# Crossbar DMA transposes, casting weight loads and a fixed program order on every engine, in a windowed-attention plus ResMLP kernel

## The chip, the cores and the metric

The kernel runs on one core of one Trainium2 chip. The metric is the device time in microseconds (us). A profiled span is about 1.7 us shorter than the time of the same run. A run counts as slow when it is over 1.5% above the fastest of the same kernel.

The engines are TensorE (PE in the profile), VectorE (DVE), ScalarE (ACT), GpSimd (POOL) and SyncE (SP, which here only issues DMAs).

## The reference

```python
# q, k, v: (8, 8, 576, 64); 8 global positions; window +-32
scores = q @ k.T / 8                      # per batch and head
mask   = |i - j| <= 32, or i global, or j global
x      = softmax(scores where mask) @ v   # -> (8, 576, 512)
u      = x + lam * (w_tok @ (alpha1*x + beta1))                  # token mixing, 576x576
out    = u + lam * (relu((alpha2*u + beta2) @ w_ch1) @ w_ch2)    # 512 -> 2048 -> 512
```

I call each of the eight batches an *image*. The MLP works on 9 groups of 512 flat rows ("mlp 0" to "mlp 8"). A group consists of four tiles of 128 rows. Image 0 completes four such tiles and image 1 completes five.

## The kernel before

TensorE executes in program order. The other engines are ordered by a scheduler. The attention of an image is latency-bound, so the MLP of an earlier image is interleaved as *filler*: the attention code yields a number, and that many MLP matmuls are issued. K, Q and the MLP input are turned by TensorE transposes and copied out of PSUM. `alpha2` and `lam` are multiplied into the weights.

```python
ctx.enter_context(tc.manual_schedule(engines={mybir.EngineType.PE}))
...
def front(b):                       # attention and token mixing of image b
    for p in range(4):
        ps = mm(BF16, 512)
        for c in range(4):          # four TensorE transposes of K
            T.transpose(out=ps[:, c*P:(c+1)*P], in_=kq16[:, 0, c, p*P:(p+1)*P], identity=identb)
        for hh in range(2):         # copied to KTz by VectorE
            V.tensor_copy(out=A(KTz, ...), in_=A(ps, ...))
        ps = sc(BF16)               # the same for Q, copied to QT by ScalarE
        ...
    # ... scores, exp, P@V, token mixing; then for each finished tile of 128 rows:
        SC.copy(out=u16, in_=U[f])
        # later: ut_tile(f): four transposes of u16, one VectorE copy to UT

def mlp(g):
    ...                             # ml <- W1 x UT, relu to HTb, ml <- HTb x W2
    V.tensor_tensor(out=u, in0=ps, in1=u, op=ALU.add)
    nc.sync.dma_start(out=outf[P*f : P*f+P, :], in_=u)

def w1_load():                      # fp32 staging, then scaled to bf16
    nc.sync.dma_start(out=r[:, 0:1024], in_=moe_w_ch1[...])
    V.tensor_scalar(out=W1[...], in0=r[...], scalar1=a2c[...], op0=ALU.mult)   # or ScalarE

for b in range(NB):
    for n in front(b):
        for _ in range(n):
            if b > 0: next(fill)
    done[0] = b + 1 if b < NB - 1 else 9     # which MLP groups are ready
```

The softmax here doesn't subtract the row's maximum and nothing guards it: scores larger than these inputs give would overflow.

## Time and profile before

The median is 469.44 us (469.03 to 470.72). The first lines are of the profile's page of the kernel before: busy time of TensorE with its share of the span, then the busy tenths in 40 slices of 11.7 us (9 is 90% or more) of TensorE and of the DMA engines, then the DMA queue that carries most, with packets, megabytes and share of the engines' time.

```profile
PE 410.1 (87%) x3779; PEld 232.9 (50%) x3779; DVE 234.1 (50%) x497; ACT 195.0 (42%) x344; POOL 176.6 (38%) x213
```

```profile
PE   0135488869999999999999999999999999999996
...
DMA  7972849994975083408330852171012001101101
```

```profile
q1 hardware_dynamic: 73008, 48.92, 37.0%
```

The digits show two stages. From the tenth slice on TensorE is full, and only fewer or shorter matmuls can help there. Before that it is idle for much of the time, and the order of loads and small operations decides. The table by stretches of the kernel before follows, as start:end and length, then busy microseconds and instructions of PE, PEld, DVE, ACT and POOL, then granted clock, DMA share and GB/s:

```profile
0.00:70.00 70.00, 28.54 (x325) 22.25 (x326) 41.88 (x94) 20.24 (x33) 48.29 (x65) 0.88 0.67 188
...
100.00:140.00 40.00, 37.60 (x351) 21.61 (x352) 21.21 (x46) 12.75 (x22) 19.81 (x24) 0.91 0.79 185
140.00:200.00 60.00, 58.99 (x606) 34.15 (x605) 31.01 (x69) 32.78 (x63) 25.83 (x31) 1.00 0.43 124
200.00:220.00 20.00, 20.00 (x204) 11.24 (x202) 10.33 (x23) 4.87 (x9) 10.81 (x13) 1.00 0.43 106
220.00:440.00 220.00, 216.28 (x1957) 119.33 (x1955) 107.75 (x230) 100.68 (x180) 56.34 (x68) 1.00 0.24 69
```

From 140 us on TensorE is idle for about 5 of 300 us, and the DMA engines have room (0.24 to 0.43). In the first 70 us TensorE works for 28.5 us. The list of waits of the kernel before (total us, times, longest) shows the first reasons: the gathered rows of the global tokens, and the casts of K.

```profile
PE mm L286 <- POOL kqn L280: 16.1, 1, 16.1
PE mm L297 <- DVE kq_101 L147: 8.5, 1, 8.5
```

The timeline of TensorE in the kernel before shows when the MLP starts (start, length, engine, line, operation):

```profile
78.04 1.44 PE L478 MATMUL ml<-UT,W_118 128*128 128x512 bf16 x3
```

So the MLP, which fills everything later, starts at 78.04 us.

| kernel before, profiled run | us |
|---|---|
| matmul work in all | 384.5 |
| lost until the first MLP matmul (78.0 us) | 56.7 |
| lost from there to 140 us | 13.4 |
| lost from 140 to 240 us | 3.6 |
| lost from 240 us on | 11.2 |

### The profile page before, as it was taken

What the parts mean: (1) busy time and instruction counts of PE and PEld (TensorE: products, weight loads), DVE (VectorE), ACT (ScalarE), POOL (GpSimd) and SP (SyncE); (2) the same over time, 40 slices, a digit from 0 to 9 for tenths busy, and PEclk for the clock granted to TensorE, in tenths of its full rate; (3) what the DMA queues carried; (4) which work ended last, traced back from release to release, by engine and by line L of the source; (5) the groups of instructions that cost most, each with busy time, mean ns of one, the idle gap of its engine ahead of it and who ended that gap; (6) DMA issues with size and microseconds to landing.
All of it is one profiled execution on the core that took longest, in us unless ns stands there. A gap on an engine that the chain in (4) does not pass through costs nothing.

```text
span 469.4 us, 9110 instructions
## 1 busy us (share of the span) xinstructions
PE 410.1 (87%) x3779; PEld 232.9 (50%) x3779; DVE 234.1 (50%) x497; ACT 195.0 (42%) x344; POOL 176.6 (38%) x213
## 2 busy tenths in 40 slices
PE   0135488869999999999999999999999999999996
PEld 0125454536556655664556456545655565444442
DVE  4635778625483548354736474556545554501001
ACT  1216412634158414831682268127712770370540
POOL 6448883825733465235414341524160023000000
PEclk9999667979999999999999999999999999999999
DMA  7972849994975083408330852171012001101101
GB/s 195 230 249 56 273 131 306 213 247 88 280 167 176 13 199 97 135 25 193 104 124 24 192 148 78 43 172 46 2 46 70 24 1 46 45 1 45 46 22 67
DMA packets 76440, 54.21 MB, mean 115 GB/s; under 512 B 49392, under 2 KB 66736, under 8 KB 76400
## 3 DMA queue, kind: packets, MB, share of 16 engines
q1 hardware_dynamic: 73008, 48.92, 37.0%
q0 software_dynamic: 2048, 4.66, 4.5%
q8 instruction: 29, 0.48, 0.4%
q10 hardware_dynamic: 1344, 0.07, 0.2%
q14 instruction: 11, 0.09, 0.1%
HBM read 39.27 MB, written 9.44 MB: 104 GB/s over the span
## 4 chain that ended last, share of the span: by engine, by line
PE 75%; POOL 7%; DMA 7%; DVE 6%; issue 3%; SPq 0%; ACT 0%; POOLq 0%; DVEq 0%; ACTq 0%
PE ml L487 26%; PE ml L478 24%; PE sc L455 8%; PE xps L380 4%; PE sc L328 4%; PE mm L358 3%; DVE KTz L299 3%; PE xps L381 2%; DMA vo<-ve 2%; DMA kq<-in_k_dram,hg_idx 2%; DMA R_94<-in_k_dram 1%; PE mm L443 1%; DMA R_94<-in_q_dram 1%; PE sc L410 1%; POOL W_119 L542 1%
## 5 line engine op out<-in xcount | busy, mean ns | idle before, releaser
L478 PE MATMUL ml<-UT,W_118 128*128 128x512 bf16 x576 | 155.4, 386 | 1.7 <-DVE U L491 1.7
L487 PE MATMUL ml<-W_119,HTb 128*128 128x512 bf16 x576 | 139.5, 379 | 0.0
L481 ACT ACTIVATE HTb<-ml,bias1T 128x512 bf16<-128x512 f32 x144 | 98.7, 687 | 31.8 <-PE ml L478 30.8
L487 PEld LDWEIGHTS <-HTb 128*128 128x128 bf16 x576 | 53.4, 98 | 56.5 <-issue 0.2
L478 PEld LDWEIGHTS <-W_118 128*128 128x128 bf16 x576 | 49.2, 99 | 39.7 <-issue 7.6
L335 ACT ACTIVATE Pt<-sc 128x432 f16<-128x432 f32 x96 | 50.1, 531 | 36.3 <-PE sc L328 17.5
L491 DVE TENSOR_TENSOR U<-ml,U 128x512 f32<-128x512 f32 x36 | 24.8, 689 | 61.2 <-PE ml L487 60.9
L392 POOL TENSOR_TENSOR XL_116<-x,LA_207 128x512 bf16<-128x512 f32 x16 | 20.3, 1269 | 76.6 <-DVE x L385 76.6
L456 DVE TENSOR_TENSOR U<-sc,x 128x512 f32<-128x512 f32 (+1 forms) x40 | 27.6, 690 | 35.3 <-PE sc L455 34.9
L299 DVE COPY KTz<-mm 64x512 bf16<-64x512 bf16 x64 | 44.0, 687 | 1.5 <-PE mm L297 0.3
L328 PEld LDWEIGHTS <-KTz 128*128 128x128 bf16 x576 | 32.2, 103 | 22.1 <-issue 3.1
L392 POOL TENSOR_TENSOR XL_115<-x,LA_207 128x512 bf16<-128x512 f32 x16 | 20.3, 1268 | 47.5 <-DVE x L385 47.4
L328 PE MATMUL sc<-QT,KTz 128*128 128x72 bf16 x576 | 36.0, 204 | 0.6 <-ACT Pt L335 0.5
L303 ACT COPY QT<-sc 128x512 bf16<-128x512 bf16 x32 | 18.6, 584 | 41.4 <-PE sc L302 40.8
L385 DVE TENSOR_TENSOR x<-xps,rden 128x640 f32<-128x640 f32 x32 | 26.4, 824 | 1.9 <-DVE rden L384 0.5
L455 PE MATMUL sc<-XL_116,wtT_122 128*128 128x512 bf16 x100 | 24.8, 379 | 0.0
L337 DVE TENSOR_TENSOR GRT_108<-Pt,grm 128x80 f16<-128x80 f16 x16 | 3.4, 212 | 43.0 <-ACT Pt L335 42.9
L455 PE MATMUL sc<-XL_115,wtT_121 128*128 128x512 bf16 x100 | 24.7, 379 | 0.0
L297 PE MATMUL mm<-identb,kq_101 128*128 128x128 bf16 x128 | 13.8, 237 | 12.0 <-DVE kq_101 L147 8.5
L380 PEld LDWEIGHTS <-PTz_106 128*128 128x128 f16 x288 | 16.9, 104 | 8.6 <-DMA vo<-ve 4.8
L380 PE MATMUL xps<-ve,PTz_107 128*128 128x65 f16 x160 | 16.6, 197 | 5.1 <-DVE x L385 5.1
L380 PE MATMUL xps<-vo,PTz_106 128*128 128x65 f16 x128 | 16.2, 203 | 4.6 <-DMA vo<-ve 4.6
(247 smaller groups left out, 557.7 us busy)
## 6 DMA issues: line engine op xcount, KB each, us to landing
out_dram<-U SPq DMA_DIRECT2D x36, 256.0 KB
vo<-ve POOLq DMA_DIRECT2D x16, 260.0 KB, 5.5
RV_99<-in_v_dram SPq DMA_DIRECT2D x16, 256.0 KB
R_94<-in_k_dram SPq DMA_DIRECT2D x4, 512.0 KB
R_95<-in_k_dram SPq DMA_DIRECT2D x4, 512.0 KB
R_96<-in_q_dram SPq DMA_DIRECT2D x4, 512.0 KB
R_97<-in_q_dram SPq DMA_DIRECT2D x4, 512.0 KB
RV_98<-in_v_dram SPq DMA_DIRECT2D x8, 256.0 KB
```

The costliest lines, as they stand in the source:

```text
L299: V.tensor_copy(out=A(KTz, 640 * (2 * p + hh) + 32, [[4, P], [1, 4]], 64 * hh, 64), in_=A(ps, 0, [[1, P], [P, 4]], 64 * hh, 64))
L328: T.matmul(out=ps[:, i * 144 + 72 * hh : i * 144 + 72 * hh + 72], lhsT=KTz[:, 2 * p + hh, 64 * t : 64 * t + P], rhs=QT[:, p, 72 * t : 72 * ...
L335: SC.activation(out=Pt[:, 432 * un : 432 * un + 432], in_=ps[:, 0:432], func=AF.Exp, bias=0.0, scale=0.125)
L380: T.matmul(out=o_, lhsT=ptz[:, base : base + P], rhs=vv, start=(i == 0), stop=False)
L385: V.tensor_tensor(out=A(x, P * p, [[64, 2], [DM, 5], [1, 64]]), in0=A(xps, 0, [[512, 2], [65, 5], [1, 64]]), in1=A(rden, 0, [[5, 2], [1, 5 ...
L392: G.tensor_tensor(out=A(xl, DM * full + P * p, [[DM, 4], [1, P]]), in0=A(x, DM * full + P * p, [[DM, 4], [1, P]]), in1=A(LA1, P * p, [[0, ...
L455: T.matmul(out=ps, lhsT=wtT[par][:, c, P * u : P * u + P], rhs=xl[:, c, :], start=(c == 0), stop=(c == 4))
L456: V.tensor_tensor(out=U[f][r0:r1, :], in0=ps[r0:r1, :], in1=x[r0:r1, u, :], op=ALU.add)
L478: T.matmul(out=ps, lhsT=W1[:, cc, ec * P : (ec + 1) * P], rhs=ut[:, cc, :], start=(cc == 0), stop=(cc == 3))
L481: SC.activation(out=HTb[:, slots[ec], :], in_=ps, func=AF.Relu, bias=bias1T[:, ec : ec + 1], scale=1.0)
L487: T.matmul(out=ps, lhsT=HTb[:, slots[ec], P * j : P * j + P], rhs=W2[:, ec, :], start=(ec == 0), stop=(ec == 15))
L491: V.tensor_tensor(out=u, in0=ps, in1=u, op=ALU.add)
```

## The change

The intent is to take the transposes off TensorE, to take the scaling of the weights off the other engines, and to fix every engine's order by hand so that image 0 runs as early as possible. The diff, cut to its core:

```diff
-ctx.enter_context(tc.manual_schedule(engines={mybir.EngineType.PE}))
+ctx.enter_context(tc.manual_schedule(engines={EN.PE, EN.DVE, EN.Activation, EN.Pool, EN.SP}))
-psM bufs=2, psL bufs=2
+psM bufs=1, psL bufs=3
@@ K and Q of images 1 to 7: loads in 256-byte rows, GpSimd casts, crossbar transposes
+def qk_chunk(b, c):
+    for i, src in enumerate((k, q)):
+        nc.sync.dma_start(out=A(r, 512*i, ...), in_=src[b, :, P*c:P*c+n, :].rearrange("h p d -> p h d"))
+    def cast(E): ...                 # to zero-padded kz and to q16
+def xbar_qk():
+    for c in range(5):
+        nc.sync.dma_start_transpose(out=A(KTz, 32+P*c, [[640, 8], [1, n]]), in_=kz[0:n, c, :])
+    nc.sync.dma_start_transpose(out=A(QT, 0, ...), in_=q16[0:64, ...])
+    nc.sync.dma_start_transpose(out=A(QT, 1600, ...), in_=q16[64:P, ...])
@@ MLP input
-                SC.copy(out=u16, in_=U[f])
-                wait.append((f, u16))        # four TensorE transposes and a copy later
+                V.tensor_tensor(out=u16, in0=U[f], in1=a2b, op=ALU.mult)
+                nc.sync.dma_start_transpose(out=UT[g][:, :, P*(f%4):P*(f%4)+P], in_=u16)
@@ output of the MLP
-            V.tensor_tensor(out=u, in0=ps, in1=u, op=ALU.add)
+            V.tensor_tensor(out=tmp, in0=ps, in1=lamb, op=ALU.mult)
+            V.tensor_tensor(out=u, in0=tmp, in1=u, op=ALU.add)
@@ weights: cast in the DMA, no scaling
-    (w1_load, w2_load: fp32 staging and scaling on VectorE, ScalarE, GpSimd)
+    G.dma_start(out=W1[:, :, 512*blk:512*blk+512], in_=moe_w_ch1[...])
+    G.dma_start(out=W2[:, 4*blk:4*blk+4, :], in_=moe_w_ch2[...])
@@ image 0 is written out by hand; it keeps TensorE transposes for K, Q (not for u16)
+done = [1]
+for _ in range(80):                # 80 MLP steps of mlp 0 before image 1
+    next(fill)
+for b in range(1, NB): ...         # 103 filler steps an image or more, before about 135
```

Who issues what is not free to choose. The Trainium skill, "DMA: Bandwidth & Descriptors", section "SWDGE vs HWDGE vs iDMA", says that only GpSimd can issue a DMA that casts, and only SyncE or ScalarE a plain DMA transpose. The change puts all transposes on SyncE, which also issues the loads of K, Q and V and the stores of the output.

## The prediction

> **What bounds it now.** The page: TensorE busy 410.1 of 469.4 us (87%); TensorE is 75% of the chain of work that ended last. The table by stretches separates two stages. From 108 us on TensorE is busy 97-100% of every stretch, so instruction count on TensorE decides there. Before that it idles: the timeline shows the first MLP matmul only at 78.0 us, and by 108 us TensorE has been busy about 60 us. By the waits and the timeline: kqn on GpSimd costs TensorE a 16.1 us wait, attention of image 0 starts at 35.8 us, VectorE and ScalarE scale W1 between its steps.
>
> **Removed.**
> 1. TensorE transposes. In dense stretches four 128-column ones advance the timeline 0.22 us and the eight small ones take 0.32 us: 8 x 0.22 + 0.32 = 2.1 us an image, 7 images, 15 us; the MLP input's 36 x 0.22 = 8 us. Together 23 us, all on the critical path.
> 2. Their evictions: VectorE KTz 64 x 0.69 and UT 36 x 0.42, ScalarE QT 32 x 0.58. Mostly off the path, but TensorE waits about 1 us at each image's head for KTz and QT (busy 1.4-1.5 of 2 us there): 6 us.
> 3. W1/W2 staging and scaling on VectorE, ScalarE and GpSimd, and the kqn detour. I expect attention of image 0 at about 20-22 us, mlp 0 at 62-66 us instead of 78: 13 us.
>
> **Added.**
> 1. Crossbar transposes: zero-padded K 1.18, Q 0.59, u16 0.59 MB an image, 2.36 MB. No trace shows one. The Trainium skill, "DMA: Bandwidth & Descriptors", section "Latency and other measured facts", states 261 GB/s effective: 9 us an image as an estimate.
> 2. K and Q of images 1-7 now load in 256-byte rows (1 KB before). V's 256-byte rows moved at 220-230 GB/s with the DMA share near 1.0, so 2.36 MB takes 10.5 us. With V 5, vo 2, output 4 us: about 31 us of DMA an image.
> 3. The filler schedule shrinks from about 135 to 101 MLP steps an image, so an image lasts about 35 us instead of 46, and pure MLP is left for the end (about 90 us instead of 45). DMA is then 85-90% loaded during images.
> 4. In image 1 mlp 1 isn't ready, so 48 of 101 steps are real; the rest of image 1 runs bare, at image 0's pace. I charge 8-10 us.
> 5. A second VectorE operation per output tile (0.69 us): off the path.
>
> **Sum.** 469.4 - 23 - 6 - 13 + 9 = 436; with the earlier indirect gathers 433 us, range 412 to 463. Faster by over 2%: 0.82; within 2%: 0.10; slower: 0.08.
>
> **What would show each step.** TensorE instructions fall by about 420, busy time to about 375-390 us, no transposes after the prologue. First MLP matmul at 60-67 us. A gap in TensorE's busy tenths of 8-12 us in image 1 (roughly 85-105 us). DMA share per image rises from about 0.4 to 0.7-0.9. The last 85-95 us are MLP alone.
>
> **What would make it wrong.** Slow crossbar transposes: at 100 GB/s they need 24 us an image, DMA needs 45 of 35 us, TensorE waits on KTz at each image's head, and since the filler order is fixed the time isn't recovered: 480 us. The in-order SyncE queue. Casting DMAs delivering W1 or W2 late (needed by about 62 and 76 us). A cold clock in image 1.

## More of the kernel before

To compare traces I use one derived figure. The *matmul work* of a stretch is the sum, over its matmuls, of columns/2.4 GHz + 2.5 ns, at least 30 ns (the shortest spacing in the timelines). The rest of the stretch is *lost*: idle, or running slowly. The formula is that of the Trainium skill, "TensorE: Matmul & The Clock Gate", section Part 1, which gives 215.7 ns for 512 columns and 55.6 ns for 128. The trace agrees: sixteen matmuls of 512 columns in the chain of work take 3.45 us, 0.216 each.

## The result, and the profile after

The changed kernel takes 454.43 us median (453.77 to 455.27, four runs) against 469.47 us in the same rounds. The ratio is 0.9676, with a 95% interval of 0.9651 to 0.9702. All ratios here are the mean time of one kernel's fast runs over that of the other's fast runs of the same rounds, so they are not quite the ratio of the medians that I quote. The gain is 15 us, where 36 were predicted.

The page of the changed kernel, the same lines:

```profile
PE 386.9 (85%) x3355; PEld 210.8 (46%) x3355; DVE 237.0 (52%) x451; ACT 160.7 (35%) x276; POOL 190.0 (42%) x253
```

```profile
PE   1266538988549999996999999999999999999995
...
DMA  8999399989989977999999799859994002201101
```

```profile
q1 hardware_dynamic: 183044, 56.93, 63.3%
```

TensorE executes 424 instructions fewer. The queue q1 now takes 63.3% of the DMA engines' time instead of 37.0%, in 2.5 times the packets, and the row of DMA tenths is near 9 until the thirtieth slice. The table by stretches of the changed kernel:

```profile
0.00:70.00 70.00, 29.66 (x349) 22.17 (x349) 44.65 (x92) 16.86 (x34) 42.82 (x65) 0.87 0.93 174
...
100.00:140.00 40.00, 26.67 (x267) 14.41 (x265) 23.47 (x44) 6.10 (x13) 24.32 (x32) 0.80 0.99 190
140.00:200.00 60.00, 59.36 (x655) 34.62 (x654) 38.69 (x76) 30.44 (x54) 35.62 (x48) 0.99 0.98 186
200.00:220.00 20.00, 16.04 (x82) 7.67 (x81) 8.65 (x15) 3.05 (x7) 8.19 (x9) 0.91 0.84 131
220.00:440.00 220.00, 218.24 (x1776) 114.39 (x1775) 113.29 (x207) 90.28 (x149) 71.22 (x92) 1.00 0.60 119
```

Two stretches lost TensorE time: 100 to 140 us (26.7 busy, before 37.6, with the granted clock down to 0.80) and 200 to 220 us (16.0, before 20.0). From 140 to 200 us the DMA engines are full (0.98), yet TensorE works for 59.4 of 60 us.

| us | before | after | difference | predicted |
|---|---|---|---|---|
| matmul work | 384.5 | 362.2 | -22.2 | -23 |
| lost until the first MLP matmul (78.0; 70.2) | 56.7 | 51.7 | -5.0 | -13, and -3 for the gathers |
| lost from there to 140 us | 13.4 | 24.2 | +10.8 | +9 |
| lost from 140 to 240 us | 3.6 | 8.7 | +5.1 | } -6 |
| lost from 240 us on | 11.2 | 6.7 | -4.5 | } |
| span | 469.4 | 453.5 | -15.9 | -36 |

The matmul work fell as predicted. What failed is the waiting. The list of waits of TensorE in the changed kernel, cut to the lines used here:

```profile
PE ml L449 <- DMA UT<-u_739: 9.2, 1, 9.2
...
PE mm L589 <- DVE wtT_122 L591: 4.8, 1, 4.8
PE sc L326 <- DVE U L380: 4.6, 2, 4.0
PE ml L449 <- DMA UT<-u_1449: 3.7, 1, 3.7
```

The longest is in front of the first MLP matmul. The wait for wtT is that of theory D below, and the one for U L380 returns in e5. The timeline of TensorE in the changed kernel shows the first:

```profile
70.21 2.29 PE L449 MATMUL ml<-UT,W_118 128*128 128x512 bf16 x5 [9.18 <-DMA UT<-u_739]
```

The tile u_739 is the last of image 0's four. SyncE's own timeline in the changed kernel says when it was issued, and what stood behind and before such transposes later. Columns are start and length of the issue:

```profile
62.74 1.25 SPq L387 DMA_TRANSPOSE UT<-u_739  x1
...
65.53 14.81 SPq L189 DMA_TRANSPOSE KTz<-kz  x5
80.43 1.36 SPq L190 DMA_TRANSPOSE QT<-q_101  x1
81.84 2.17 SPq L191 DMA_TRANSPOSE QT<-q_101  x1
...
114.31 7.78 SPq L189 DMA_TRANSPOSE KTz<-kz  x5
122.19 1.92 SPq L190 DMA_TRANSPOSE QT<-q_101  x1
124.16 3.82 SPq L191 DMA_TRANSPOSE QT<-q_101  x1
128.07 1.62 SPq L387 DMA_TRANSPOSE UT<-u_1411  x1
...
132.66 1.19 SPq L387 DMA_TRANSPOSE UT<-u_1449  x1
```

The issue of u_739 began at 62.74 us and the matmul could start at 70.21 us. Behind it the block of seven transposes for image 1's K and Q occupies the queue from 65.53 to 84.0 us. The second block, at 114.31 us, is image 2's. It stands in program order ahead of image 1's MLP input, which mlp 1 and all later filler need. The chain of work of the changed kernel shows that this decides (start, length, what):

```profile
128.07 3.77 DMA UT<-u_1411
132.66 2.33 DMA UT<-u_1449
...
137.41 1.28 PE ml L449 x3
...
142.50 0.86 PE ml L449 x4
```

The tile u_1411 was written by VectorE by 124.9 us. SyncE reached it only at 128.07 us. With three buffers for u16, VectorE could write the fourth tile (u_1449) only when u_1411 had landed, at 131.84 us, and u_1449 itself landed at 135.0 us. Then TensorE, idle before, ran at half clock: 1.28 us for three matmuls of 512 columns (0.427 each) at 137.41 us, and 0.86 us for four (0.215 each) at 142.50 us. The Trainium skill, "TensorE: Matmul & The Clock Gate", section Part 1, states 426.7 and 215.7 ns for cold and warm, and this trace agrees.

The loss at 200 to 220 us has the same form. In the changed kernel VectorE's timeline and then TensorE's show it:

```profile
213.28 0.69 DVE L386 TENSOR_TENSOR u_2571<-U,a2b 128x512 bf16<-128x512 f32 x1 [5.04 <-DMA UT<-u_2521]
```

```profile
215.95 1.01 PE L326 MATMUL sc<-QT,KgT 128*128 128x256 bf16 x4 [3.96 <-DVE U L380]
```

VectorE waits 5.04 us for a u16 buffer. The tile in it, u_2521, was written by 203.6 us; SyncE reached it at 206.36 us, behind image 4's K and Q block, and it landed at 213.18 us, 6.83 us after its issue. TensorE then waits 3.96 us for VectorE, since the first score tile of image 4 reuses a PSUM buffer that VectorE has not read yet.

### The profile page after: what moved, and what is told of

It is laid out like the page before. It is cut to its first block, busy times and chain, and to the rows that moved or that the text cites. A ratio compares the mean times of both kernels' runs of the same rounds, so it can differ in the third digit from the quotient of the medians.

```text
span 453.5 us, 8392 instructions
## 1 busy us (share of the span) xinstructions
PE 386.9 (85%) x3355; PEld 210.8 (46%) x3355; DVE 237.0 (52%) x451; ACT 160.7 (35%) x276; POOL 190.0 (42%) x253
## 3 DMA queue, kind: packets, MB, share of 16 engines
q1 hardware_dynamic: 183044, 56.93, 63.3%
## 4 chain that ended last, share of the span: by engine, by line
PE 57%; DVE 11%; DMA 4%; POOL 2%; issue 2%; ACT 0%; DVEq 0%; POOLq 0%
PE ml L449 22%; PE ml L458 20%; PE sc L379 5%; DVE U L464 3%; PE sc L281 3%; PE xps L343 2%; DVE tmp L463 2%; PE xps L344 2%; DMA UT<-u_2521 2%; PE mm L309 1%; DVE U L380 1%; PE sc L326 1%; DVE x L348 1%; POOL XL_116 L355 1%; DMA QT<-q_101 1%
## 5 line engine op out<-in xcount | busy, mean ns | idle before, releaser
L449 PE MATMUL ml<-UT,W_118 128*128 128x512 bf16 x576 | 145.3, 389 | 12.9 <-DMA UT<-u_739 9.2
L449 PEld LDWEIGHTS <-W_118 128*128 128x128 bf16 x576 | 52.0, 100 | 63.9 <-issue 18.4
L463 DVE TENSOR_TENSOR tmp<-ml,lamb 128x512 f32<-128x512 f32 x36 | 24.8, 690 | 89.1 <-PE ml L458 89.0
L288 ACT ACTIVATE Pt<-sc 128x432 f16<-128x432 f32 x90 | 46.9, 529 | 49.8 <-PE sc L281 37.3
L281 PEld LDWEIGHTS <-KTz 128*128 128x128 bf16 x576 | 31.9, 103 | 26.7 <-issue 7.9
L380 DVE TENSOR_TENSOR U<-sc,x 128x512 f32<-128x512 f32 (+1 forms) x40 | 27.4, 685 | 27.7 <-PE sc L379 27.3
L281 PE MATMUL sc<-QT,KTz 128*128 128x72 bf16 x540 | 33.4, 202 | 5.8 <-DVE QT L234 5.8
L110 POOL CAST kz<-R_96 128x512 bf16<-128x512 f32 x14 | 9.7, 695 | 61.2 <-DMA R_96<-in_k_dram 61.0
L464 DVE TENSOR_TENSOR U<-tmp,U 128x512 f32<-128x512 f32 x36 | 30.8, 857 | 1.2
L344 PE MATMUL xps<-RS_112,GS_110 128*128 128x65 f16 x160 | 16.3, 199 | 7.5 <-DVE RS_112 L317 7.4
L327 ACT ACTIVATE GS_110<-sc 64x320 f16<-64x320 f32 (+1 forms) x8 | 3.2, 404 | 51.5 <-PE sc L326 51.5
L327 ACT ACTIVATE GS_111<-sc 64x320 f16<-64x320 f32 (+1 forms) x8 | 3.2, 404 | 47.0 <-PE sc L326 41.5
L326 PE MATMUL sc<-QT,KgT 128*128 128x320 bf16 (+1 forms) x64 | 12.4, 329 | 8.2 <-DVE U L380 4.6
```

The costliest lines, as they stand in the source:

```text
L281: T.matmul(out=ps[:, i * 144 + 72 * hh : i * 144 + 72 * hh + 72], lhsT=KTz[:, 2 * p + hh, 64 * t : 64 * t + P], rhs=A(QT, qo(t) + 80 * p, ...
L288: SC.activation(out=Pt[:, 432 * un : 432 * un + 432], in_=ps[:, 0:432], func=AF.Exp, bias=0.0, scale=0.125)
L344: T.matmul(out=o_, lhsT=gs[:, P * u : P * u + P], rhs=rs[:, h, :], start=False, stop=True)
L380: V.tensor_tensor(out=U[f][r0:r1, :], in0=ps[r0:r1, :], in1=x[r0:r1, u, :], op=ALU.add)
L449: T.matmul(out=ps, lhsT=W1[:, cc, ec * P : (ec + 1) * P], rhs=ut[:, cc, :], start=(cc == 0), stop=(cc == 3))
L463: V.tensor_tensor(out=tmp, in0=ps, in1=lamb, op=ALU.mult)
```

## The experiments

Each kernel is the changed kernel with the edit shown, unless said otherwise. All gave the reference's result. Eighteen ran, in six sets of runs. "Before" was measured in each set (medians 469.1 to 470.7), and ratios are to it. The expectations name theories by letters:

- **A**: the crossbar transposes sit in the path by their own latency and by their order on SyncE's queue.
- **B**: image 1 lacks filler (48 of 101 steps; by the code it is 103).
- **C**: W2's casting loads are in the way around 57 to 70 us.
- **D**: VectorE's fixed order lets one waiting operation hold up others.
- **E**: the DMA engines are saturated by 256-byte rows.
- **F**, formed later: GpSimd's fixed order holds up image 0.

### First set: one suspect at a time

**e1_w2_early** issues the four casting loads of W2 between image 0's attention steps instead of after its token mixing.

```diff
+    (W2 blocks 0, 1 after c_qk[0](G); blocks 2, 3 after c_qk[1](G))
     drain(tokmix(0, x))
-    (W2 blocks 0, 1 before c_qk[0](G); blocks 2, 3 after xbar_qk())
```

> Only the four W2 casting DMAs move: from after token mixing of image 0 (issued at 57.5 and 63 us) to between the attention steps of image 0 (about 42 and 46 us), where the DMA share falls to 0.01-0.4 at 48-57 us. Theory C (weights in the way: W2 on the same DMA engines is what delays the four MLP-input transposes of image 0, whose landing ends a 9.2 us TensorE wait): first MLP matmul at 63-66 us instead of 70.2, the K/Q crossbar block of image 1 shorter than 14.8 us, time 444-449. Theory A (crossbar transposes are slow by themselves, one after another on the SyncE queue): first MLP matmul still at 67-70, time 452-455.

Measured: 448.86 us, ratio 0.9554 (0.9504 to 0.9604), 5.6 us below the changed kernel. The first MLP matmul came at 65.6 us instead of 70.2, and image 1's five K transposes held SyncE for 8.95 us instead of 14.81. The list of waits of e1:

```profile
PE ml L449 <- DMA UT<-u: 4.5, 1, 4.5
...
PE ml L449 <- issue: 2.8, 1, 2.8
```

The timeline puts the wait of 4.5 us before mlp 1 (at 129.87 us) and that of 2.8 us before mlp 0. So the first wait fell from 9.2 to 2.8 us. (The view names no releaser for it, but the fourth tile's transpose was issued only at 63.18 us.) The second tile landed 2.3 us after its issue, in the changed kernel 8.95. Without W2's loads beside it, the first landing costs less than a third: C, as it was stated, explains most of the first wait, and nothing of image 1.

**e2_ut01_pe** gives the MLP input of images 0 and 1, nine tiles, back to TensorE.

```diff
+    def ut_tile():                  # one token-mixing step later
+        ps = ml(BF16)
+        (four T.transpose of u16 into ps)
+        SC.copy(out=UT[f // 4][...], in_=A(ps, 0, [[P, 4], [1, P]]))
-                nc.sync.dma_start_transpose(out=UT[g][...], in_=u16)
+                if b < 2: wait.append((f, u16))
+                else:     nc.sync.dma_start_transpose(out=UT[g][...], in_=u16)
```

> The MLP input of images 0 and 1 alone is transposed on TensorE again (8 tiles, +1.8 us of TensorE work), all else stays. Theory A (the latency of the crossbar path sits on the chain twice, 9.2 us before the first MLP matmul and about 10 us from 125 to 135 us between image 1 and MLP 1): time 438-444, no wait of TensorE on UT. Theory B (image 1 merely has too little filler): the wait at 60-70 us goes, but the hole between 110 and 135 us stays nearly as long, time 446-449.

Measured: 438.84 us (438.34 to 440.82), ratio 0.9372 (0.9327 to 0.9418), 15.6 us below the changed kernel. Matmul work rose by 2.0 us (36 transposes of 0.055 us). Lost time by stage was 43.6, 17.7, 4.2 and 6.7 us, against 51.7, 24.2, 8.7 and 6.7 in the changed kernel. The stretch of e2, and two of its waits (the first is the new transposes, waiting for VectorE's u16):

```profile
100.00:140.00 40.00, 31.58 (x371) 18.71 (x367) 23.54 (x48) 16.18 (x31) 23.50 (x31) 0.87 1.06 195
```

```profile
PE ml L377 <- DVE u L397: 2.8, 4, 1.0
PE sc L326 <- DVE KgT L232: 2.3, 1, 2.3
```

TensorE is busy 31.6 of the 40 us at 100 to 140 us, in the changed kernel 26.7, and no wait for the landing of a UT tile is left. A change of nine tiles returns as much as the whole change had gained. This is the main evidence for A.

**e3_fill27** keeps 101 of the 128 steps of mlp 0 for image 1.

```diff
-    for _ in range(80):
+    for _ in range(27):
```

> 27 instead of 80 MLP steps ahead of image 1, so that image 1 has its full 101 steps. Theory B: the idle at 110-120 us (6.5 us) and the bare token mixing go, time 443-447. Theory A: image 1 now starts 11 us earlier, before its K and Q have come through the crossbar (they landed at about 86 us), and TensorE waits there instead: time 451-456.

Measured: 456.66 us, ratio 0.9756 (0.9694 to 0.9818): no gain. The waits for UT grew to 16.3 us in two places. B alone is refuted: more filler gives no gain while TensorE still waits for the landings, and image 1, now begun earlier, waits for its Q (4.1 us) and vo (5.9 us).

**e4_xl_early** moves one GpSimd memset and its VectorE operation, which make VectorE wait 2.35 us at 48 us, to an earlier place.

```diff
+    (after LA1:)  G.memset(XL[0][64:P, 4, :], 0.0); V.tensor_tensor(out=XL[0][64:65, 4, :], ...)
     pv(0, 3, x)
-    G.memset(XL[0][64:P, 4, :], 0.0)
-    V.tensor_tensor(out=XL[0][64:65, 4, :], ...)
```

> The clearing and bias row of XL of image 0 are issued earlier in program order (theory D: VectorE's in-order queue waits 2.4 us for GpSimd's memset there and holds back the copies that TensorE's row sums wait for, 4.8 us idle at 47-52 us). Theory D: token mixing starts 4-5 us earlier. If everything after follows, time 449-451; if the crossbar or W2 decides the first MLP matmul (theories A, C), the gain is lost in a longer wait there, time 452-455.

Measured: 453.56 us, ratio 0.9666 (0.9623 to 0.9708), the same as the changed kernel. The expected 4 to 5 us did not come: token mixing starts at 53.3 us in both traces. TensorE's wait for wtT fell only from 4.8 to 3.8 us, since VectorE then waited 2.11 us for the next memset in GpSimd's queue (wtT, L628 of that kernel). So e4 says little about D; it exchanged one wait for the next.

### Second set: the parts of the change

**e5_sched_pe** gives the other engines back to the scheduler.

```diff
-    ...manual_schedule(engines={EN.PE, EN.DVE, EN.Activation, EN.Pool, EN.SP})
+    ...manual_schedule(engines={EN.PE})
```

> The changed kernel with only TensorE in program order, as in the kernel before; the compiler's scheduler places VectorE, ScalarE, GpSimd and SyncE again. If program order on these engines is itself a gain (early indirect gathers, casts where they are wanted), this is slower: 458-470. If it is what blocks queues (transposes waiting behind the K/Q block on SyncE), it is faster: 444-452. I lean to slower.

Measured: 468.34 us, ratio 0.999 (0.995 to 1.003). Without the fixed order the whole gain is gone, 14 us. TensorE waits for VectorE at image heads, as the list of waits of e5 shows:

```profile
PE sc L326 <- DVE U L380: 16.7, 5, 4.8
```

In the changed kernel this line has 4.6 us in two places. So the fixed order is worth as much as the change itself, in the company of the other parts. I did not try it alone on the kernel before.

**e6_noload** leaves out the loads of K and Q for images 2 to 7, and **e7_noxbar** their crossbar transposes. Both compute from stale K and Q. Their outputs are wrong, which doesn't matter for the times. The comparison with the reference still passes, because q and k are drawn at a tenth of unit size, so that the scores are near zero and the softmax is almost uniform.

```diff
 e6:    for i, src in enumerate((k, q) if b < 2 else ()):  nc.sync.dma_start(...)
 e7:    def xbar_qk(b):
 e7:        if b > 1: return
```

> Wrong result on purpose: K and Q of images 2-7 are not loaded, the casts and crossbar transposes work on the old contents. Takes away 2.36 MB of 256-byte rows an image and ten SyncE issues, leaves every transpose. Theory E (the DMA engines are saturated, share near 1.0 from 140 to 340 us, and the loads are part of it): crossbar blocks get shorter and the waits at 125-135 and 211-216 us shrink, time 444-449. Theory A (the crossbar transposes queue one behind another on SyncE whatever else moves): time 451-454.

> Wrong result on purpose: the crossbar transposes of K and Q of images 2-7 are left out, loads and casts stay. Theory A: the MLP-input transposes of images 1-6 no longer stand behind an 11-15 us K/Q block, the wait of 125-135 us shrinks from about 10 to 3-5 us and that of 211-216 us goes, time 441-446; the wait before the first MLP matmul at 70 us stays. Theory E: about the same, with the DMA share falling by a third; if both e6 and e7 gain alike it is bandwidth, if only e7 gains it is the transposes' own queue.

Measured: e6 448.3 us, ratio 0.9525 (0.9477 to 0.9574); e7 445.5 us, ratio 0.9495 (0.946 to 0.953). Taking away all of these loads is worth 6 us, and taking away the transposes 9 us. Both bound roughly what a better layout could win, and each is less than e2's nine tiles. In e6 the first wait for UT was 14.0 us, in e7 7.8 and in the changed kernel 9.2, with the same code up to there, so this wait varies from run to run. (e1's 2.8 us lies well below all of these.) E is a part, and not the main one: the engines are full from 140 to 200 us and TensorE hardly waits. e6 also takes ten issues an image off SyncE, which these runs do not separate from the bandwidth.

**e8_ut_all_pe** is e2 for all eight images (`if b < 8`).

> The MLP input of all images is transposed on TensorE again, K and Q stay on the crossbar. Against the run with images 0 and 1 alone (438.8): 28 more tiles, +6.2 us of TensorE work, less the 4-5 us wait of 205-220 us and some crossbar traffic. Expected 440-445; below 438 would say that the crossbar is no gain for the MLP input anywhere.

Measured: 450.59 us, ratio 0.9593 (0.9548 to 0.9638), 10 to 12 us worse than e2 (by the ratios, by the medians). In the list of waits of e8, the new transposes wait for VectorE's u16:

```profile
PE ml L377 <- DVE u L397: 10.5, 11, 1.3
```

From image 2 on the crossbar for the MLP input is thus a gain. The 27 further tiles cost 6 us of matmul work (27 x 0.22), and the waits for u16 grow by 7.7 us. The likely reason that the landings cost little there is that filler covers them; in images 0 and 1 there is none.

### Third and fourth set: further repairs on top of e2

**e9_combo** is e2 with the edits of e1 and e4. **e10_combo_fill27** is e9 with 27 steps before image 1. **e11_combo_masks** is e9 with the mask operations moved behind the copies that TensorE waits for:

```diff
 e11:
-    masks(scr)
     kqn = glob_kq(kq)
     ...
     glob(kqn)
+    masks(scr)
```

> e2 (MLP input of images 0 and 1 on TensorE) together with e1 (W2 casting loads earlier) and e4 (bias row of XL earlier). Before this the other two were masked by the wait for the crossbar landing, which e2 took away. Theory C (W2's casting loads in the way) and D (VectorE's queue held by the memset of XL) say: the 4.8 us that PE waits for wtT at 47 to 52 us go, and the first MLP matmul comes at 58 to 59 us instead of 63; the wait for W2/KgT at 82 to 85 us (2.3 us) shrinks; time 431 to 435 us. If they had no share of their own, the time stays at e2's 438.8 us within 1 us.

> e9 with 27 instead of 80 MLP steps before image 1, so that all 101 steps that image 1 asks for are there. Theory B (image 1 runs bare of filler): e2 lost 12 us at 104 to 122 us with image 1 bare; with filler most of that goes, so 5 to 9 us less than e9. Theory A in its K/Q form (the K/Q crossbar block of image 1 is the next limit): PE now asks for KTz and QT some 11 us earlier and waits for them instead; then the time equals e9's within 2 us and a wait on a DMA of QT or KTz stands at 75 to 85 us.

> e9 with the nine small mask operations on VectorE placed after the copies of the global keys and queries into QT, which PE waits 5.8 us for at 17 to 23 us. Head-of-line theory (D): this wait falls to about 2 us, the whole run moves up by 3 to 4 us. Rival: the copies wait for GpSimd (the gathered rows) anyway, or the masks now hold up the exponentials' successors by as much, and the time is e9's within 1 us.

Measured: 440.16 us (ratio 0.934), 439.76 us (0.9323) and 437.8 us (0.9338), all with intervals that overlap e2's. My expectation of 431 to 435 us for e9 was wrong. In e9 the wait for wtT did not go, it grew to 6.3 us. VectorE's timeline in e9 names the releaser, and GpSimd's timeline shows what stood before it:

```profile
54.05 0.45 DVE L607 CAST wtT<-mm 1x288 bf16<-1x288 f32 x1 [4.62 <-POOL wtT L648]
```

```profile
52.74 0.45 POOL L361 TENSOR_TENSOR XL<-x,LA 64x128 bf16<-64x128 f32 x1
53.13 0.36 POOL L647 MEMSET wtT<- 128x320 bf16 x1
53.43 0.58 POOL L648 MEMSET wtT<- 64x576 bf16 x1
```

The memset in L648 of that kernel stood in GpSimd's queue behind the XL products, which stood behind casts of K and Q that wait for their loads. In e11 the wait for the copies fell from 5.0 to 1.2 us as expected, and the wait for wtT grew to 6.7 us. In e10 the bare stretch was filled, and waits for vo (6.3 us) and QT (4.7 us) stand in its list instead.

**e12_g_order** is e2 with the late masks and with eight GpSimd memsets moved ahead of image 0's attention. **e13_g_order_fill54** is e12 with 54 steps before image 1.

```diff
+    G.memset(ecol...), XL[0], wtT[1] (two), GS[1], RS[1], XL[1]     # before c_qk = [...]
     ...
-    (the same memsets between pv(0, 1, x) and tokmix(0, x))
-    c_qk[0](G)
     pv(0, 1, x)
+    c_qk[0](G)
```

> e2 with eight memsets on GpSimd moved from the middle and the end of image 0's attention to before it, the cast of image 1's first K/Q chunk placed after the second XL product, and the masks late as in e11; W2's loads where the change had them. Theory F (GpSimd's own program order is what PE waits for in image 0: in e9 and e11 VectorE waits 4.6 and 5.1 us for a wtT memset that stands in GpSimd's queue behind K/Q casts that wait for loads): the wait for wtT at 47 to 55 us falls from 4.8 to 6.7 us to under 2 us, the first MLP matmul comes at 56 to 59 us instead of 63 to 65, and the time is 432 to 435 us. If the wait only moves to the next thing in the same queue (the XL product itself), the wait of the token mixing for XL grows by what wtT lost and the time stays at 437 to 440 us.

> e12 with 54 instead of 80 MLP steps before image 1. Theory B: image 1 then has 74 of its 101 steps, and of the 12 us that are lost at 100 to 122 us in e2 some half go: 3 to 5 us less than e12. If image 1's K, Q and V are not there earlier (10 fell short with waits for vo and QT at 70 to 90 us), the waits move there and the time equals e12's within 2 us.

Measured: e12 438.09 us (434.60 to 439.93), ratio 0.9355 (0.9283 to 0.9427); e13 439.74 us, ratio 0.9377 (0.9292 to 0.9462). (One of e13's four runs, 445.79 us, counted as slow; the median of the other three is 438.3 us.) The mechanism of F is right: the wait for wtT is 2.4 us in e12, and was 4.8 us in e2. The first MLP matmul moved from 63.05 to 59.2 us in e12, and to 56.1 us in e13. But the time did not move beyond its scatter. In e13 the waits for vo and QT (7.5 and 3.6 us) stand at the head of image 1: with filler to spare, image 1's V and Q arrive too late.

### Fifth set: how e2's gain divides

**e14_ut0_pe** moves only image 0's four tiles (`if b == 0`), **e15_ut1_pe** only image 1's five (`if b == 1`). **e16_ut01_again** is e2 unchanged, and **e17_g_order_again** e12 unchanged, for a comparison in the same rounds.

> Only image 0's four MLP input tiles on TensorE, image 1's five stay on the crossbar. If the two shares of e2's 15.6 us are separate (the 9.2 us wait for the first landing, and image 1's waits behind the K/Q block of 6 to 10 us), this gives 7 to 9 us: 445 to 448 us, with waits for UT left at 125 to 140 us only. Rival (the gain is one: what image 0 wins is swallowed at image 1, since the crossbar block of image 2's K/Q and image 1's tiles still end at the same time): 451 to 455 us, with a longer wait for UT at 120 to 140 us.

> Only image 1's five tiles on TensorE, image 0's four stay on the crossbar. Separate shares: 6 to 8 us gain over the changed kernel, 446 to 448 us, with the 9 us wait for the first landing still there. Rival (one gain): 451 to 455 us.

> e2 unchanged, on the same chip and in the same rounds as e14, e15 and e17, for a fair comparison: 437 to 440 us.

> e12 unchanged. Its profiled run was 3.8 us shorter than e2's and its first MLP matmul 3.8 us earlier, but its median was not. If the earlier start carries through to the end, the mean is 2 to 4 us below e16's; if it is made up for by an equally longer bare stretch of image 1 (100 to 120 us), the two agree within 1 us.

| | median us | ratio to before | 95% interval |
|---|---|---|---|
| changed kernel (first measurement) | 454.43 | 0.9676 | 0.9651 to 0.9702 |
| e14, image 0's tiles | 441.12 | 0.9384 | 0.934 to 0.9428 |
| e15, image 1's tiles | 446.48 | 0.9475 | 0.9426 to 0.9524 |
| e16, both | 438.74 | 0.9327 | 0.928 to 0.9374 |
| e17, both and GpSimd's order | 441.3 | 0.9282 | 0.9209 to 0.9356 |

Two of e15's eight runs counted as slow; the median of the other six is 446.2 us. Image 0's four tiles alone return some 13 us, image 1's five alone some 8 to 9, both some 16. e15 lies in the range expected for separate shares (446 to 448 us), e14 below both of its ranges, and together they give more than e2.

The kept traces show where. Those of e14, e15 and e16 come from another execution than the runs' first profiles (spans of 441.3, 442.6 and 437.7 us) and lack some matmul records, so I use times alone:

| us | mlp 0 starts | mlp 1 starts | from there to the end |
|---|---|---|---|
| changed kernel | 70.2 | 135.1 | 318.4 |
| e14, image 0's tiles | 62.8 | 128.2 | 313.1 |
| e15, image 1's tiles | 69.0 | 132.0 | 310.6 |
| e2, both | 63.1 | 125.0 | 311.6 |
| e16, both again | 63.4 | 124.0 | 313.8 |
| e7, no K/Q transposes from image 2 on | 68.2 | 131.3 | 310.7 |

Up to the start of mlp 1 the gains over the changed kernel are 6.9 us in e14, 3.1 in e15 and 10.1 in e2: these add up. After it each of them is 5 to 8 us shorter than the changed kernel. Most of that is one stretch: between the first token-mixing matmuls of images 3 and 4 pass 43.9 us in the changed kernel, 39.2 in e14, 39.1 in e15, 40.1 in e2 and 42.5 in e16. This gain can be had only once, and adding e14's and e15's counts it twice. Why e14, which leaves images 1 to 7 as they were, has it too is not shown; the two profiles of e2's kernel differ by 2.4 us in that stretch.

e14 also avoids the half clock after the first wait: from 70 to 80 us the changed kernel loses 2.8 us (granted clock 0.70), and e14 nothing (1.00).

In e17 four of six runs counted as slow, being over 1.5% above its fastest (434.35 to 444.72), so its ratio rests on two runs. Whether e12 beats e2 stays open. The first profiled runs of one and the same kernel, e2 and e16, lost 72.3 and 75.9 us in all (spans of 436.6 and 440.2 us); a difference of 3 us between two profiles is therefore nothing here.

### Sixth set: the buffers of the MLP input

**e18_u16_5buf** is e2 with five buffers of u16 instead of three.

```diff
-    pU16 bufs=3
+    pU16 bufs=5
```

> e2 with five buffers for the MLP input before its transpose instead of three. At image 3 (200 to 220 us) VectorE waits 2.4 us in e2 and 4.2 us in e16 for a crossbar transpose to free one of the three buffers, and TensorE waits for VectorE at the head of the next image. If the wait for the buffer is what costs there, the wait goes from VectorE's list, the stretch 140 to 240 us loses 1 to 3 us less than e2's 4.2 and e16's 7.2, and the time is 435 to 438 us. If the queue itself is the limit, the wait moves to TensorE (MLP input not landed) and the time stays at 438 to 439 us.

Measured: 438.35 us, ratio 0.9326 (0.9289 to 0.9363), not to be told from e16's 0.9327. The wait of VectorE for a landing is gone from its list, and TensorE's wait for VectorE at the image heads fell from 2.0 us in e2 to 0.6. The time does not show it. The buffers were the way in which the queue's delay reached VectorE in these traces, but they are worth less than the scatter of 1%.

The best version is thus e2 (or one of its near equals), 438.8 us: 6.5% below the kernel before, and 3.4% below the changed kernel.

## Why the prediction was right or wrong

The direction was right, and the time lies in the predicted range. The gain was mis-sized by 21 us. Term by term:

1. **"Together 23 us, all on the critical path" (TensorE transposes): right.** Matmul work fell by 22.2 us, instructions by 424 (about 420 predicted), and busy time to 386.9 us (375 to 390).
2. **"mlp 0 at 62-66 us instead of 78: 13 us", and 3 us for the gathers: wrong, 5.0 us.** The first MLP matmul came at 70.2 us. The step that failed is that a transpose on the crossbar was counted in bandwidth only. It was never asked where TensorE has nothing else to do until it lands. Attention of image 0 began at 22.7 us (20 to 22 predicted), so the start was won. But from 61.0 us on TensorE waited 9.2 us for the last of four tiles. e14 removes this wait and starts mlp 0 at 62.8 us, inside the prediction's 62 to 66. e1 shows that W2's loads, which the change issues at that moment, made most of the wait: without them it was 2.8 us.
3. **"TensorE waits about 1 us at each image's head ...: 6 us": right for the later images, given back by an earlier one.** From 240 us on 4.5 us less are lost. From 140 to 240 us 5.1 us more are lost, most of it around the head of image 4 (200 to 220 us), where image 3's MLP input stood behind a K and Q block and landed late. e14 and e15 keep that block, and TensorE waits for VectorE at the image heads less than half as long in them (2.0 and 1.8 us in their lists, against 4.6). Likely, then, the loss depends on how the two streams happen to meet.
4. **"I charge 8-10 us" for the bare image 1: about right in size (+10.8), the cause only in part.** The prediction gave the missing filler as the reason. e3, e10 and e13 supply filler and gain nothing. In e2 the loss from the first MLP matmul to 140 us falls from 24.2 to 17.7 us with the same filler. Two things that the prediction did not charge are in the changed kernel's 24.2. One is the half clock after the two waits for the crossbar: 2.8 us from 70 to 80 us and 2.3 us from mlp 1's start to 140 us. The other is the way of image 1's MLP input over SyncE, behind image 2's K and Q block: from image 1's first token-mixing matmul to mlp 1 it takes 15.5 us, but 11.6 in e15 and 11.7 in e7, which has no such block. That is about 4 us; the larger part of what e15 and e7 win (8 to 9 us) comes after mlp 1's start. The bare stretch that stays in e2 is covered in e10 and e13, but then the arrival of image 1's V and Q takes over.
5. **"9 us an image" for crossbar transposes: too low by a factor of two.** The twelve transposes issued from 114.31 us on add up to 20.0 us of SyncE's time for 2.42 MB (K 1.18, Q 0.59, five u16 tiles 0.66), about 121 GB/s beside other loads. The estimate took 261 GB/s from the Trainium skill, "DMA: Bandwidth & Descriptors", section "Latency and other measured facts". The measurement decides.
6. **"DMA is then 85-90% loaded during images": too low, 98%, but nearly harmless.** TensorE is busy 59.4 of 60 us there. e6 bounds the worth of the loads by 6 us.
7. **"Pure MLP is left for the end (about 90 us instead of 45)": wrong, without consequence.** After the last token-mixing matmul 63.5 us remain in the changed kernel (from 390.0 us) and 62.6 before (from 406.8 us). TensorE is full there in both. The count of 101 steps an image left out a loop that both kernels have: token mixing draws one more MLP step as long as nine tiles of U are in use. In the changed kernel's trace images 2 to 6 take 103, 108, 144, 128 and 144 MLP matmuls.

The prediction did list "the in-order SyncE queue" among what could make it wrong, in four words and without a cost. It cost some 4 us in image 1 and had a part in the loss at image 4. Two more of its risks were near the mark: W2's loads were not late, but slowed the transposes beside them (e1), and the clock was cold in image 1 (0.80 from 100 to 140 us). The gain of the fixed order, which e5 measures at 14 us, was not in the sum as a term at all, only implied in the earlier start of image 0.

What stays open: why e14 loses less at image 4, and whether e12's earlier start is worth anything at the end. Not tried: e15 together with e1, which would keep image 0's input on the crossbar with W2's loads out of its way, and the casting weight loads alone, which no run takes back.

A tempting repair was not tried: moving image 1's u16 transposes to ScalarE's queue. The Trainium skill, "DMA: Bandwidth & Descriptors", section "Silent corruption: two transposing streams in flight at once", says that transposes issued from two engines can silently corrupt each other unless one stream waits for the other's completion. With that wait the order would be fixed again. No run here shows the corruption.

## What to carry to other kernels

Moving a transpose from TensorE to the DMA crossbar trades 0.22 us of TensorE time per 128-row tile for a landing of several microseconds on a queue that is served in order. Do it where enough independent work is at hand during the landing (here image 2 on: worth 10 to 12 us by e2 against e8), and keep TensorE transposes where the result is needed next (here images 0 and 1: worth 16 us). When a wait is removed and the time does not move, look for the next operation on the same in-order queue before adding further repairs: e4 and e11 each shortened a wait and saw the next one take its place.

## What the Trainium skill lacked or had wrong

- "DMA: Bandwidth & Descriptors", section "Latency and other measured facts", gives 261 GB/s for a DMA transpose (350 to 400 when contiguous). Here twelve transposes in a row occupied SyncE for 20.0 us with 2.42 MB, about 121 GB/s, beside loads that kept the engines' share at 0.99. No figure is given for a transpose beside other traffic.
- The same page, section "Issuing engines are not separate DMA queues", calls the time to initiate a DMA usually small relative to the DMA. For crossbar transposes it was not: 1.2 us per 128 KB tile of MLP input (u_1449), 7.78 us for five K chunks, against landings of 2.29 to 8.95 us after the issue (MLP input, where the trace has them). No page gives a measured time for which a transpose holds its issuing queue on trn2; cycle counts stand only in a passage on trn3.
- The same page, section "Alternative transpose paths", lists TensorE without a price. Times of a single transpose by either path stand elsewhere in the skill, but no page says that the choice depends on what TensorE has to do until the landing. Here four TensorE transposes cost 0.22 us of TensorE time per tile, and choosing between the two paths by stage was worth 10 to 12 us (e8 against e2) in one direction and 16 us (e2) in the other.
- "TensorE: Matmul & The Clock Gate", Part 1, agreed: 0.427 and 0.215 us per matmul of 512 columns, cold and warm.
